# Splitting a weight-conversion step into two moves and laying attention's steps out anew, in a kernel of attention and two feed-forward layers

## The chip, the cores and the metric

The kernel runs on one core of a Trainium2 chip. The metric is the device time of one execution in microseconds; the kernel before was run three times.

## What is computed

The inputs are float64. For each of 8 batches and 8 heads an attention is computed between 512 tokens `x` and 32 states, in both directions; the two results, laid side by side, are 4352 rows of 512. They pass through two feed-forward layers of width 2048, the first with a leaky slope `alpha`, the second with `h - tanh(h)`:

```
xread = softmax(scale * x @ state.T) @ state
sread = softmax(scale * state @ x.T) @ x
x  = concat([xread, sread])              # 8 batches of 512 + 32 rows
h  = x @ w_in;  g = max(h, 0) + alpha * min(h, 0);  x = g @ w_out
h  = x @ w2_in; out = (h - tanh(h)) @ w2_out
```

## The kernel before

**Products in parts.** Each operand of a large product is held as a high and a low part, and a product is three matmuls of 128x512 (`TERMS`, L32).

**The first layer** goes by blocks of 512 rows, one per batch, and by 16 slices `f` of 128 hidden columns; one (block, slice) is a *visit*, and (1,4) below is slice 4 of block 1. `emit_h` (L581) makes the hidden slice: 12 matmuls in block 0, and 6 in blocks 1 to 7, where it reads a product of w_in with the batch's states (`PW`) instead of w_in. `act_a` (L595) makes the activation and its high part `g` (ScalarE L598, VectorE L599, ScalarE L600), `act_b` (L603) the low part (VectorE L604), and `emit_o` (L609) sends the visit *before* through w_out in 12 matmuls (L619). The order of visits is block 0, slices 0 to 7; block 1, slices 0 to 15; block 0, slices 8 to 15; then the other blocks (L1160).

**A visit is a list of places.** Around those calls stand lists of small tasks, kept in `plan` by `at(i, f, place, ...)` (L1018), in this order: `emit_h`, *early*, `act_a`, *gap*, *mid*, `emit_o` of the visit before, *late*, *end* (L1162 to L1183). `act_b` stands between gap and mid in blocks 1 to 7, and behind mid in block 0. Every engine works through its own share of this one order; within a place, tasks run as they were added.

**The conversion** turns the float64 weights of the first layer into two float32 words, 32 jobs of 512 KB (`jobs`, L125). A step (`conv_step`, L176) number t does a phase of five jobs: `conv_a` of job t-1 (ScalarE, L112), `conv_b` of t-2 (VectorE L115, L117, L118, the last one adding the sign, and ScalarE L122), `conv_load` of t (a DMA on SP's queue, L103 or L109), `conv_c` of t-3 (ScalarE copy L159 or L161, GpSimd add L162) and `conv_d` of t-4 (GpSimd subtract L168 or L171, which completes the part). There are 36 steps: six before the first visit, 17 in block 0's first eight visits (two or three in each), 13 in block 1. Raw words lie in a ring of four buffers (tag `raw`); a buffer is free once L118 and L122 have read it. The ring also takes two of the four reads of `PW` for block 1 (L366).

**Attention** of a batch goes by two groups of heads, `a` and `c`, in steps s0 to s6 whose places `timetable` (L1021) lists: transposes on TensorE (s0, s1, s3b, s6), scores (s2), the softmax on VectorE and ScalarE (s2t, s2b, s3, s3x, s4, s4m, s4t), the split into the operand of `emit_h` (s4b) and the states' read (s5). `state_mask` and `state_turn` (L336, L343) prepare the states, `project_one` (L389) makes half a product of w_in with the states: three matmuls into a PSUM tile (L396), high part by ScalarE (L399), low part by VectorE (L400), and two DMAs of 256 KB to memory; `load_parts` (L404) reads them back. All these small products use a PSUM pool of two tiles (`ps_a`, L61), handed out in turn.

Of the kernel before, what the change touches and what calls it, by code (L numbers as in the profile page):

```python
# [35 lines left out]
def attention_and_two_mlps(ctx, tc, x, state, w1_in, w1_out, alpha, w2_in, w2_out, out):  # L36
    nc = tc.nc
    B, H, S, D = x.shape
# [5 lines left out]
    NF = DFF // P  # L44
# [66 lines left out]
    def high_abs(m, r):  # L111
        nc.scalar.activation(m.bitcast(F32), r[:, :, 1].bitcast(F32), AF.Abs)  # L112

    def high_word(m, r):
        nc.vector.tensor_scalar(m.bitcast(F32), m.bitcast(F32), HIGH_MAX, HIGH_MIN,  # L115
                                op0=ALU.min, op1=ALU.max)
        nc.vector.tensor_scalar(m, m, 3, LOW30, op0=ALU.logical_shift_left, op1=ALU.bitwise_and)  # L117
        nc.vector.scalar_tensor_tensor(m, r[:, :, 1], SIGN_TOP, m,  # L118
                                       op0=ALU.bitwise_and, op1=ALU.bitwise_or)

# [6 lines left out]
    raws, words, low, loaded = {}, {}, {}, set()  # L127
# [10 lines left out]
        high_abs(words[k], raws[k])  # L138

    def conv_b(k):  # L140
        r = raws.pop(k)
        high_word(words[k], r)
        low[k] = work.tile([P, DM], I32, tag="cq", name="cq", bufs=3)
        low_word(low[k], r)

# [25 lines left out]
            nc.gpsimd.tensor_tensor(w_out(f, 1), v, w_out(f, 0).bitcast(F32), op=ALU.subtract)  # L171

    ticks = [0]
    phases = [conv_load, conv_a, conv_b, conv_c, conv_d]

    def conv_step():  # L176

        t = ticks[0]
        if t >= 2 * NF + 4:
            return  # L180
        for lead in (1, 2, 0, 3, 4):
            if 0 <= t - lead < 2 * NF:
                phases[lead](t - lead)
        ticks[0] += 1

# [5 lines left out]
    def combine(mat, j, take, ahead):  # L193

        def raw(m, jj):
            got = []
            for h in range(2):
                r, done = take("raw")
                raw_words(r, 1, jj + h * NJ, m)
                got.append((r, done))  # L200
            return got

        got = ahead.pop((mat, j), None)
        if got is None:
            got = raw(mat, j)
        m, m_done, q, q_done = [], [], [], []

        def a(h):
            t, done = take("m")
            m.append(t)  # L210
            m_done.append(done)
            high_abs(t, got[h][0])

        def b(h):
            high_word(m[h], got[h][0])
            t, done = take("q")
            q.append(t)
            q_done.append(done)
            low_word(t, got[h][0])
            got[h][1]()  # L220

        def c(h):
            nc.gpsimd.tensor_tensor(q[h], m[h], q[h], op=ALU.add)  # L223
            m_done[h]()

        a(0)
        yield
        a(1)
        b(0)
        yield  # L230
        b(1)
        c(0)
        yield
        c(1)
        n = (mat, j + 1) if j + 1 < NJ else (mat + 1, 0)
        if n[0] < 2:
            ahead[n] = raw(*n)
        yield "words"
        u, v = (t.bitcast(F32) for t in q)
        s, s_done = take("s")  # L240
        one, two = slice(0, HW), slice(HW, DM)
        sub = partial(nc.gpsimd.tensor_tensor, op=ALU.subtract)

        def parts(src, places):
            n = src.shape[-1]
            o, done = take("o")
            o = o[:, :, :n]
            nc.scalar.copy(o[:, 0], src)  # L248
            yield
            sub(o[:, 1], src, o[:, 0].bitcast(F32))  # L250
            for k, i in enumerate(places):
                nc.sync.dma_start(out=wc_dram[mat][j // 2][i, j % 2], in_=o[:, :, k * HW:(k + 1) * HW].bitcast(F32))
            done()

        if mat == 0:
            nc.gpsimd.tensor_tensor(s[:, one], v[:, one], v[:, two], op=ALU.add)
            sub(v[:, one], u[:, one], v[:, one])
            yield from parts(u, (0, 5))
            sub(s[:, two], v[:, two], v[:, one])
            yield from parts(v, (4, 6))  # L260
            sub(u[:, two], u[:, two], s[:, two])
            yield from parts(s, (1, 2))
            yield from parts(u[:, two], (3,))
        else:
            sub(s[:, one], u[:, one], u[:, two])
            sub(u[:, one], v[:, one], u[:, one])
            yield from parts(v, (3, 5))
            sub(s[:, two], v[:, one], s[:, one])
            yield from parts(u, (4, 0))
            sub(v[:, two], v[:, two], s[:, two])  # L270
            yield from parts(s, (1, 2))
            yield from parts(v[:, two], (6,))
        s_done()
        for done in q_done:
            done()
# [742 lines left out]
    def at(i, f, when, *todo):  # L1018
        plan.setdefault((i, f, when), []).extend(todo)

    def timetable(i, a, c):  # L1021

        if i == 0:
            when = dict(s0=(1, "gap"), s1=(2, "early"), s2=2, s2t=2, s2b=2, s3=2, s3x=(2, "late"),
                        s3b=(3, "early"), s4=3, s4m=3, s4t=3, s4b=(3, "late"), s5=(3, "late"), s6=(4, "late"))
            then = dict(s0=(4, "gap"), s1=(5, "early"), s2=5, s2t=5, s2b=5, s3=5, s3x=(5, "late"),
                        s3b=(6, "early"), s4=6, s4m=6, s4t=6, s4b=(6, "late"), s5=(6, "late"), s6=(7, "late"))
        else:
            def table(first):
                return dict(s0=first, s1=first + 1, s2=first + 2, s2t=(first + 3, "gap"), s2b=first + 3,  # L1030
                            s3=(first + 4, "gap"), s3x=first + 4, s3b=(first + 4, "late"), s4=(first + 5, "gap"),
                            s4m=first + 5, s4t=(first + 6, "gap"), s4b=(first + 6, "late"), s5=first + 6,
                            s6=(first + 7, "late"))
            start = 7 if i + 2 < B else 5
            when, then = (table(0), table(start)) if i > 1 else (table(9), table(8 + NF))
        for g, table in ((a, when), (c, then)):
            for name, w in table.items():
                f, place = w if isinstance(w, tuple) else (w, "mid")

                at(*((i, f) if f < NF else (0, f - NF + (NF // 2 if g is a else 0))), place, getattr(g, name))  # L1040

    with tc.manual_schedule():
        load_next_x()
# [7 lines left out]
        for z in [a.spread, a.s0, a.s1, tick, a.s2, c.spread, a.s2t, c.s0, a.s3, c.s1, a.s3x, c.s2, c.s2t, c.s3,  # L1051
                  a.s4, c.s3x, tick, a.s4m, a.s4t, c.s4, tick, tick, c.s4m, c.s4t, a.r0, a.r1, tick,
                  c.r0, c.r1, slopes, tick, load_next_x, load_next_x]:
            z()
        at(0, 0, "gap", a.s2b)
        at(0, 0, "late", c.s2b)
        at(0, 1, "early", a.s3b, c.s3b)
        at(0, 1, "late", a.s5)
        at(0, 2, "gap", c.s5)
        at(0, 2, "late", a.s6, c.s6)  # L1060
        places = dict(gap=(0, 2, 4, 6), mid=(1, 3, 5, 7), late=(0, 2, 4, 6), end=(0, 1, 3, 5, 7))
        for f, place in ((0, "gap"), (0, "end"), (1, "gap"), (2, "gap"), (2, "end"), (3, "gap"), (4, "gap"), (4, "end"),
                         (5, "gap"), (6, "gap"), (7, "late"), (8, "gap"), (9, "gap")):
            at(1, f, place, tick)
        for place, fs in places.items():
            for f in fs:
                at(0, f, place, tick)
        a = attention(1, 0)
        turns = [(0, 1, 0, (0, "mid"), (1, "early")), (0, 2, 0, (1, "mid"), (2, "early")),
                 (0, 1, 1, (2, "end"), (3, "early")), (0, 2, 1, (3, "mid"), (4, "early"))]  # L1070
        for i in (2, 4, 6):
            turns += [(i, i + 1, 0, (0, "early"), (0, "late")), (i, i + 1, 1, (2, "late"), (3, "late"))]
            if i + 2 < B:
# [13 lines left out]
            at(i, f, "early", partial(state_mask, b, g, True))  # L1087
            at(i, f, "end", partial(state_turn, b, g, scores=False))
        todo = [(1, q, g) for q in range(NF // FQ) for g in range(NG)]
        places = [(0, 4), (0, 5), (0, 7), (1, 0), (1, 2), (1, 3), (1, 5), (1, 6)]  # L1090
        todo += [(b, q, g) for b in (3, 5, 7) for g in range(NG) for q in range(NF // FQ)]
        places += [(0, f) for f in range(8, NF)] + [(2, f) for f in range(NF)]
        for (b, q, g), (i, f) in zip(todo, places):
# [1 line left out]
            at(i, f, "late", partial(project_one, b, q, g, 1))  # L1095
        for k in range(2 * NF // FQ):
            at(*((0, 9 + 2 * k) if k < 4 else (2, 2 * k - 7)), "end", partial(save_w_in, k // 2, k % 2))
        for q, (i, f, place) in enumerate(((0, 6, "early"), (1, 2, "early"), (1, 6, "late"), (1, 9, "late"))):
            at(i, f, place, partial(load_parts, 1, q))
        at(0, 10, "late", load_half_sum)  # L1100
        for i, (blk, n) in enumerate(seq):
# [54 lines left out]
        for f in range(6, NF):  # L1156
            at(B, f, "late", partial(fill.go, 1))

        pend = None
        visits = [(0, f) for f in range(NF // 2)] + [(1, f) for f in range(NF)] + [(0, f) for f in range(NF // 2, NF)]  # L1160
        visits += [(i, f) for i in range(2, len(seq)) for f in range(NF)]
        for i, f in visits:  # L1162
# [4 lines left out]
            g = act_a(n, f, ph)  # L1167
            for z in plan.get((i, f, "gap"), ()):
                z()
            if 0 < i < B:  # L1170
                act_b(n, f, ph, g)
            for z in plan.get((i, f, "mid"), ()):
                z()
            if not 0 < i < B:
                act_b(n, f, ph, g)
            if pend:
                emit_o(*pend)
# [123 lines left out]
```

## Time and profile before

| | us |
|---|---|
| median of three runs | 1522.1 (1518.54 to 1523.98) |
| profiled execution, its own time | 1523.92 |
| span of its instructions | 1522.1 |
| first matmul of visit (0,0) | 29.59 |
| first matmul of visit (1,0) | 118.45 |
| first matmul of visit (1,9) | 192.39 |

The span is what the trace covers; all times of the trace count from its start. An idle time before an instruction is followed by what ended it: `[3.09 <-DMA raw]` is 3.09 us of idle, ended by the landing of a transfer.

### The profile page before, as it was taken

To read this page: it belongs to the slowest core of one execution; us is meant where nothing else is said; L and a number is where in the kernel's file an instruction comes from. 1 tells how busy PE (TensorE), PEld (TensorE's weight loads), DVE (VectorE), ACT (ScalarE), POOL (GpSimd) and SP (SyncE) were. 2 spreads that over 40 slices of the span, in tenths; PEclk is the share of its full clock that TensorE was granted. 3 is DMA by queue.
4 is the path that set the end of the run, shared out by engine and by line. 5 is a ranking of instruction groups with operands and counts; after the bars stand their busy time and mean duration, and the time that the engine had idled before them with its cause. 6 is when DMAs were issued, how large, how long until landed. Compare 5 with 4: busy or idle time off the path is not lost.

```text
span 1522.1 us, 22868 instructions
## 1 busy us (share of the span) xinstructions
PE 1427.7 (94%) x8188; PEld 1194.2 (78%) x8188; DVE 980.7 (64%) x1430; ACT 729.2 (48%) x1322; POOL 530.7 (35%) x414
## 2 busy tenths in 40 slices
PE   5777799989999999999999899999999999999998
PEld 2555577766677677777988687888888989999998
DVE  6876544656577666676445565656347688878874
ACT  4655534444455555555434454545345444444443
POOL 2544400000145445435300211112016387666662
PEclk9998799999999999999999999999999999999999
DMA  6357707795769596758972767272796943443421
GB/s 163 121 167 230 219 2 266 250 318 162 203 189 250 170 263 199 224 172 267 285 223 87 280 208 249 111 271 105 253 344 210 346 132 133 139 139 132 139 84 35
DMA packets 230977, 294.40 MB, mean 193 GB/s; under 512 B 57808, under 2 KB 133584, under 8 KB 229840
## 3 DMA queue, kind: packets, MB, share of 16 engines
q1 hardware_dynamic: 228608, 292.39, 59.9%
q8 instruction: 64, 1.05, 0.3%
q10 hardware_dynamic: 2256, 0.56, 0.2%
q14 instruction: 49, 0.40, 0.1%
HBM read 170.73 MB, written 122.16 MB: 192 GB/s over the span
## 4 chain that ended last, share of the span: by engine, by line
PE 60%; DVE 6%; DMA 5%; ACT 4%; issue 3%; POOL 2%; SPq 1%; ACTq 0%; DVEq 0%; POOLq 0%
PE ps_m L987 20%; PE ps_m L806 17%; PE acc L619 12%; PE ps_h L591 6%; PE ps_m L871 2%; DVE ps_h L599 1%; DVE g L604 1%; PE ps_p L396 1%; ACT g L600 1%; ACT t L598 1%; DMA c_raw<-in_moe_w_in 1%; DMA rx<-y 1%; DMA gt<-g 1%; DMA g<-t 1%; DVE c L823 1%
## 5 line engine op out<-in xcount | busy, mean ns | idle before, releaser
L619 PE MATMUL acc<-g,wo 128*128 128x512 f32 (+1 forms) x1728 | 424.3, 393 | 23.3 <-ACT g L600 12.0
L619 PEld LDWEIGHTS acc<-g,wo 128*128 128x128 f32 x1728 | 316.8, 194 | 110.6 <-DVE g L604 18.7
L987 PE MATMUL ps_m<-wp,s 128*128 128x256 f32 x2856 | 343.0, 282 | 2.9 <-ACT e L970 2.8
L987 PEld LDWEIGHTS ps_m<-wp,s 128*128 128x128 f32 x2856 | 341.4, 190 | 4.6 <-ACT e L970 3.2
L806 PE MATMUL ps_m<-x,ch 128*128 128x512 f32 x1344 | 312.6, 394 | 8.3 <-DVE c L823 4.5
L806 PEld LDWEIGHTS ps_m<-x,ch 128*128 128x128 f32 x1344 | 251.8, 188 | 68.6 <-DVE c L823 6.5
L932 DVE TENSOR_TENSOR s<-gt,s 128x512 fp32r<-128x512 f32 (+1 forms) x216 | 219.4, 1067 | 44.3 <-ACT s L948 43.4
L599 DVE SCALAR_TENSOR_TENSOR ps_h<-ps_h,sign,t 128x512 f32<-128x512 f32 (+1 forms) x144 | 104.8, 727 | 158.3 <-ACT t L598 157.8
L600 ACT ACTIVATE g<-ps_h,sign 128x512 fp32r<-128x512 f32 (+1 forms) x144 | 95.7, 665 | 152.0 <-DVE ps_h L599 152.0
L591 PE MATMUL ps_h<-x,pw 128*128 128x512 f32 x624 | 163.5, 397 | 4.2 <-DMA pw<-pw 4.2
L948 ACT CAST s<-gt 128x512 fp32r<-128x512 f32 (+1 forms) x216 | 120.4, 597 | 88.9 <-PE ps_m L987 37.3
L598 ACT ACTIVATE t<-ps_h,slope 128x512 f32<-128x512 f32 (+1 forms) x144 | 95.7, 664 | 98.9 <-PE ps_h L591 98.6
L604 DVE SCALAR_TENSOR_TENSOR g<-ps_h,sign,g 128x512 fp32r<-128x512 f32 (+1 forms) x144 | 102.7, 713 | 59.5 <-ACT g L600 56.6
L591 PEld LDWEIGHTS ps_h<-x,pw 128*128 128x128 f32 x624 | 114.6, 189 | 29.9 <-issue 5.0
L223 POOL TENSOR_TENSOR c_q<-c_m,c_q 128x512 int32<-128x512 int32 x32 | 42.1, 1315 | 268.6 <-ACT c_q L122 218.9
L817 POOL TENSOR_TENSOR t<-c,t 128x512 f32<-128x512 f32 x32 | 41.6, 1300 | 251.8 <-ACT t L816 224.1
L816 ACT ACTIVATE t<-c 128x512 f32<-128x512 f32 x96 | 60.5, 632 | 123.1 <-DVE c L823 108.7
L823 DVE TENSOR_TENSOR c<-ps_m,c 128x512 f32<-128x512 f32 x96 | 64.7, 685 | 58.7 <-PE ps_m L806 43.2
L250 POOL TENSOR_TENSOR c_o<-c_q,c_o 128x512 fp32r<-128x512 f32 (+1 forms) x48 | 54.4, 1134 | 108.7 <-ACT c_o L248 108.7
L914 POOL TENSOR_TENSOR s<-gt,gt 128x512 f32<-128x512 f32 (+1 forms) x36 | 54.8, 1525 | 84.4 <-DMA gt<-g 83.9
L817 DVE TENSOR_TENSOR t<-c,t 128x512 f32<-128x512 f32 x64 | 53.9, 842 | 46.6 <-ACT t L816 46.6
L162 POOL TENSOR_TENSOR cq<-cm,cq 128x512 int32<-128x512 int32 x32 | 41.6, 1301 | 102.6 <-DVE cm L118 56.2
(138 smaller groups left out, 1643.0 us busy)
## 6 DMA issues: line engine op xcount, KB each, us to landing
g<-t SPq DMA_DIRECT2D x128, 256.0 KB, 2.3
gt<-g SPq DMA_DIRECT2D x64, 512.0 KB, 5.1
wc<-c_o SPq DMA_DIRECT2D x112, 256.0 KB, 3.3
ch<-wc SPq DMA_DIRECT2D x56, 512.0 KB, 7.6
pw<-pw SPq DMA_DIRECT2D x104, 256.0 KB, 5.2
wp<-wc SPq DMA_DIRECT2D x28, 512.0 KB, 7.5
raw<-in_moe_w_in SPq DMA_DIRECT2D x16, 512.0 KB, 4.7
raw<-in_moe_w_out SPq DMA_DIRECT2D x16, 512.0 KB, 5.1
```

The source lines that it names most:

```text
L591: nc.tensor.matmul(ps[:, :n], lhsT=w[i], rhs=xt[:, j, :n], start=(k == 0 and m == 0), stop=(k == len(pairs) - 1 and m == 2))
L598: nc.scalar.mul(t, ph, slope[:, f:f + 1])
L599: nc.vector.scalar_tensor_tensor(ph, ph, sign[:, f:f + 1], t, op0=ALU.mult, op1=ALU.max)
L600: nc.scalar.mul(g[:, 0, :n], ph, sign[:, f:f + 1])
L604: nc.vector.scalar_tensor_tensor(g[:, 1, :n], ph, sign[:, f:f + 1], g[:, 0, :n].bitcast(F32), op0=ALU.mult, op1=ALU.subtract)
L619: nc.tensor.matmul(acc[t][:, :n], lhsT=w[i][:, t * P:(t + 1) * P], rhs=g[:, j, :n], start=(first and k == 0), stop=(last and k == 2))
L806: nc.tensor.matmul(b, lhsT=w[p][:, cc], rhs=XT[key, i][cc][:, q], start=(i not in GOES_ON and cc == k == 0), stop=(cc == 1 and k == 2), sk ...
L817: eng.tensor_tensor(t, h, t, op=ALU.subtract)
L823: nc.vector.tensor_tensor(h, ps[j, i], h, op=ALU.add)
L932: nc.vector.tensor_tensor(made[k - 1][:, 1], src, made[k - 1][:, 0].bitcast(F32), op=ALU.subtract)
L948: nc.scalar.copy(made[k][:, 0], source(blk, i, jj))
L987: nc.tensor.matmul(dst[:, t * HW:(t + 1) * HW], lhsT=s[:, p, r, t * P:(t + 1) * P], rhs=w[:, q], start=first, stop=(jj == NJ // 2 - 1 and ...
```

## The change

The step becomes two moves. The first does L112, L115 and L117 and the load, and the load is now that of job t+1. The second does L118 and L122 (`conv_s`), `conv_c` and `conv_d`. In block 0 each of the first eight visits gets two steps, at early and gap and at late and end; block 1 gets 14 steps over its first eleven visits, two each in slices 2, 3 and 4. `act_b` stands ahead of mid in block 0 too (its slices 8 to 15 included). Batch 1's attention, the states' turns, six of the eight projections for block 1 and its four reads of `PW` are placed elsewhere.

```diff
-    def high_word(m, r):
+    def high_word(m):
...
+    def sign_word(m, r):
         nc.vector.scalar_tensor_tensor(m, r[:, :, 1], SIGN_TOP, m,
...
     def conv_b(k):
+        high_word(words[k])
+
+    def conv_s(k):
         r = raws.pop(k)
-        high_word(words[k], r)
+        sign_word(words[k], r)
         low[k] = work.tile([P, DM], I32, tag="cq", name="cq", bufs=3)
         low_word(low[k], r)
...
-    phases = [conv_load, conv_a, conv_b, conv_c, conv_d]
+
+    def moves(*phases):
+        t = ticks[0]
+        if t < 2 * NF + 4:
+            for phase, lead in phases:
+                if 0 <= t - lead < 2 * NF:
+                    phase(t - lead)
+
+    def conv_step_a():
+
+        moves((conv_a, 1), (conv_b, 2), (conv_load, -1))
+
+    def conv_step_b():
+        moves((conv_s, 2), (conv_c, 3), (conv_d, 4))
+        ticks[0] += 1
 
     def conv_step():
-
-        t = ticks[0]
-        if t >= 2 * NF + 4:
-            return
-        for lead in (1, 2, 0, 3, 4):
-            if 0 <= t - lead < 2 * NF:
-                phases[lead](t - lead)
-        ticks[0] += 1
+        conv_step_a()
+        conv_step_b()
...
         if i == 0:
-            when = dict(s0=(1, "gap"), s1=(2, "early"), s2=2, s2t=2, s2b=2, s3=2, s3x=(2, "late"),
-                        s3b=(3, "early"), s4=3, s4m=3, s4t=3, s4b=(3, "late"), s5=(3, "late"), s6=(4, "late"))
-            then = dict(s0=(4, "gap"), s1=(5, "early"), s2=5, s2t=5, s2b=5, s3=5, s3x=(5, "late"),
-                        s3b=(6, "early"), s4=6, s4m=6, s4t=6, s4b=(6, "late"), s5=(6, "late"), s6=(7, "late"))
+            when = dict(s0=(2, "late"), s1=(3, "early"), s2=(3, "late"), s2t=(3, "end"), s2b=(3, "end"), s3=(3, "end"),
+                        s3x=(4, "gap"), s3b=(4, "late"), s4=(4, "end"), s4m=(4, "end"), s4t=(4, "end"), s4b=(5, "gap"),
+                        s5=(5, "early"), s6=6)
+            then = dict(s0=(5, "late"), s1=(6, "early"), s2=6, s2t=(6, "late"), s2b=(6, "late"), s3=(6, "late"),
+                        s3x=(6, "end"), s3b=7, s4=(7, "early"), s4m=(7, "early"), s4t=(7, "gap"), s4b=7, s5=(7, "late"),
+                        s6=(NF, "late"))
...
+        def halves(i, f, *places):
+            for k, place in enumerate(places):
+                at(i, f, place, (conv_step_a, conv_step_b)[k % 2])
+
+        for f in range(NF // 2):
+            halves(0, f, "early", "gap")
+        for f in range(11):
+            if f in (2, 3, 4):
+                halves(1, f, "early", "gap", "mid", "end")
+            else:
+                halves(1, f, "gap", "end")
         at(0, 0, "gap", a.s2b)
         at(0, 0, "late", c.s2b)
-        at(0, 1, "early", a.s3b, c.s3b)
-        at(0, 1, "late", a.s5)
-        at(0, 2, "gap", c.s5)
-        at(0, 2, "late", a.s6, c.s6)
-        places = dict(gap=(0, 2, 4, 6), mid=(1, 3, 5, 7), late=(0, 2, 4, 6), end=(0, 1, 3, 5, 7))
-        for f, place in ((0, "gap"), (0, "end"), (1, "gap"), (2, "gap"), (2, "end"), (3, "gap"), (4, "gap"), (4, "end"),
-                         (5, "gap"), (6, "gap"), (7, "late"), (8, "gap"), (9, "gap")):
-            at(1, f, place, tick)
-        for place, fs in places.items():
-            for f in fs:
-                at(0, f, place, tick)
+        at(0, 1, "mid", a.s3b, c.s3b)
+        at(0, 2, "mid", a.s5)
+        at(0, 2, "late", c.s5)
+        at(0, 3, "mid", a.s6, c.s6)
         a = attention(1, 0)
-        turns = [(0, 1, 0, (0, "mid"), (1, "early")), (0, 2, 0, (1, "mid"), (2, "early")),
-                 (0, 1, 1, (2, "end"), (3, "early")), (0, 2, 1, (3, "mid"), (4, "early"))]
+        turns = [(0, 1, 0, (0, "mid"), (1, "late")), (0, 2, 0, (1, "late"), (2, "early")),
+                 (0, 1, 1, (3, "mid"), (4, "early")), (0, 2, 1, (3, "late"), (4, "late"))]
...
-        places = [(0, 4), (0, 5), (0, 7), (1, 0), (1, 2), (1, 3), (1, 5), (1, 6)]
+        places = [(0, 4), (0, 5), (1, 0), (1, 1), (1, 3), (1, 4), (1, 6), (1, 7)]
...
-        for q, (i, f, place) in enumerate(((0, 6, "early"), (1, 2, "early"), (1, 6, "late"), (1, 9, "late"))):
+        for q, (i, f, place) in enumerate(((0, 7, "early"), (1, 2, "late"), (1, 6, "early"), (1, 9, "early"))):
             at(i, f, place, partial(load_parts, 1, q))
...
+        for f in range(NF // 2):
+            halves(0, f, "late", "end")
...
-            if 0 < i < B:
+            if i < B:
                 act_b(n, f, ph, g)
             for z in plan.get((i, f, "mid"), ()):
                 z()
-            if not 0 < i < B:
+            if i == B:
                 act_b(n, f, ph, g)
```

## Rows read from the trace of the kernel before

**Rows 1.** The page: busy tenths of TensorE, and its granted clock, in 40 slices.

```profile
PE   5777799989999999999999899999999999999998
...
PEclk9998799999999999999999999999999999999999
```

**Rows 2.** Busy time by stretch: first the column heads, then three stretches.

```profile
core 0: us, PE busy (x) PEld busy (x) DVE busy (x) ACT busy (x) POOL busy (x), PEclk, DMA share, GB/s
...
29.59:118.45 88.86, 65.80 (x376) 47.75 (x375) 73.10 (x132) 53.91 (x103) 46.30 (x36) 0.88 0.49 144
118.45:192.39 73.94, 57.20 (x194) 43.22 (x195) 45.54 (x70) 37.60 (x66) 32.42 (x26) 0.83 0.76 231
...
295.00:315.00 20.00, 17.21 (x75) 12.36 (x74) 9.19 (x16) 7.53 (x15) 0.00 (x0) 1.00 0.97 344
```

**Rows 3.** TensorE's longest wait in block 0's stretch, 29 to 118.4: us, times, longest.

```profile
PE ps_p L396 <- DVE wide L554: 4.4, 1, 4.4
```

**Rows 4.** TensorE's waits in block 1's stretch, 118.4 to 192.4.

```profile
PE ps_p L396 <- DVE pe L400: 7.0, 2, 4.7
PE acc L619 <- DVE g L604: 4.4, 3, 1.9
PE ps_h L591 <- DMA pw<-pw: 4.2, 2, 2.8
PE ps_w L569 <- DVE wi L400: 2.6, 1, 2.6
```

**Rows 5.** ScalarE's waits for raw words, in block 1's stretch.

```profile
ACT cm L112 <- DMA raw<-in_moe_w_out: 11.4, 5, 3.2
...
ACT cm L112 <- DMA raw<-in_moe_w_in: 2.9, 2, 1.5
```

**Rows 6.** Timeline: one load's issue, and ScalarE's wait for its landing.

```profile
136.84 0.53 SPq L109 DMA_DIRECT2D raw<-in_moe_w_out  x1
...
142.06 0.66 ACT L112 ACTIVATE cm<-raw 128x512 f32<-128x512 f32 x1 [3.09 <-DMA raw<-in_moe_w_out]
```

**Rows 7.** Groups by line and shape, 0 to 200 us: total, mean ns.

```profile
L115 DVE TENSOR_SCALAR cm<-cm 128x512 f32<-128x512 f32 x32 | 23.3, 728 | 0.0
L118 DVE SCALAR_TENSOR_TENSOR cm<-raw,cm 128x512 int32<-128x512 int32 x32 | 23.1, 722 | 1.1
...
L117 DVE TENSOR_SCALAR cm<-cm 128x512 int32<-128x512 int32 x32 | 19.4, 607 | 1.1
...
L400 DVE TENSOR_TENSOR wi<-ps_p,wi 128x512 fp32r<-128x512 f32 x8 | 5.5, 688 | 4.5 <-ACT wi L399 4.4
```

**Rows 8.** Timeline: L115 beside a GpSimd instruction, then L115 and L117 alone.

```profile
106.58 1.29 POOL L168 TENSOR_TENSOR wi<-cq,wi 128x512 fp32r<-128x512 f32 x1
106.80 1.35 DVE L115 TENSOR_SCALAR cm<-cm 128x512 f32<-128x512 f32 x1
...
114.62 0.42 DVE L115 TENSOR_SCALAR cm<-cm 128x512 f32<-128x512 f32 x1
...
115.08 0.43 DVE L117 TENSOR_SCALAR cm<-cm 128x512 int32<-128x512 int32 x1
```

**Rows 9.** Timeline: groups of 12 matmuls, at the high clock and behind an idle time.

```profile
97.75 3.00 PE L619 MATMUL acc<-g,wo 128*128 128x512 f32 x12
...
187.51 5.01 PE L619 MATMUL acc<-g,wo 128*128 128x512 f32 x12
```

**Rows 10.** DMA issues: KB each, median us from issue to landing.

```profile
raw<-in_moe_w_out SPq DMA_DIRECT2D x16, 512.0 KB, 5.1
...
wo<-pw SPq DMA_DIRECT2D x8, 256.0 KB, 8.2
```

**Rows 11.** Waits after the stretches, 192 to 420 us: TensorE's longest.

```profile
PE acc L619 <- ACT g L600: 3.1, 1, 3.1
```

**Rows 12.** Timeline: visit (0,7), its hidden slice on TensorE and its activation on VectorE.

```profile
101.27 3.07 PE L591 MATMUL ps_h<-x,wi 128*128 128x512 f32 x12
...
113.97 0.75 DVE L599 SCALAR_TENSOR_TENSOR ps_h<-ps_h,sign,t 128x512 f32<-128x512 f32 x1
```

More of the change, by code (lines that the diff above doesn't have):

```diff
@@ L214, in b @@
         def b(h):
-            high_word(m[h], got[h][0])
+            high_word(m[h])
+            sign_word(m[h], got[h][0])
             t, done = take("q")
@@ L1038, in timetable @@
                 f, place = w if isinstance(w, tuple) else (w, "mid")
-                at(*((i, f) if f < NF else (0, f - NF + (NF // 2 if g is a else 0))), place, getattr(g, name))
+                if f >= NF:
+                    j, f = (1, f - NF) if i == 0 else (0, f - NF + (NF // 2 if g is a else 0))
+                    at(j, f, place, getattr(g, name))
+                else:
+                    at(i, f, place, getattr(g, name))
     with tc.manual_schedule():
@@ L1054, in attention_and_two_mlps @@
             z()
+        def halves(i, f, *places):
[6 more added lines that the diff above has]
+                halves(1, f, "early", "gap", "mid", "end")
+            else:
+                halves(1, f, "gap", "end")
         at(0, 0, "gap", a.s2b)
         at(0, 0, "late", c.s2b)
-        at(0, 1, "early", a.s3b, c.s3b)
-        at(0, 1, "late", a.s5)
-        at(0, 2, "gap", c.s5)
-        at(0, 2, "late", a.s6, c.s6)
-        places = dict(gap=(0, 2, 4, 6), mid=(1, 3, 5, 7), late=(0, 2, 4, 6), end=(0, 1, 3, 5, 7))
-        for f, place in ((0, "gap"), (0, "end"), (1, "gap"), (2, "gap"), (2, "end"), (3, "gap"), (4, "gap"), (4, "end"),
-                         (5, "gap"), (6, "gap"), (7, "late"), (8, "gap"), (9, "gap")):
-            at(1, f, place, tick)
-        for place, fs in places.items():
-            for f in fs:
-                at(0, f, place, tick)
+        at(0, 1, "mid", a.s3b, c.s3b)
+        at(0, 2, "mid", a.s5)
+        at(0, 2, "late", c.s5)
+        at(0, 3, "mid", a.s6, c.s6)
         a = attention(1, 0)
-        turns = [(0, 1, 0, (0, "mid"), (1, "early")), (0, 2, 0, (1, "mid"), (2, "early")),
-                 (0, 1, 1, (2, "end"), (3, "early")), (0, 2, 1, (3, "mid"), (4, "early"))]
+        turns = [(0, 1, 0, (0, "mid"), (1, "late")), (0, 2, 0, (1, "late"), (2, "early")),
+                 (0, 1, 1, (3, "mid"), (4, "early")), (0, 2, 1, (3, "late"), (4, "late"))]
         for i in (2, 4, 6):
```

## The prediction
> **What bounds the kernel now.** I read the page's slices first. TensorE is busy nine tenths almost everywhere behind slice 5, and in the first five slices 5 to 7 tenths, at a granted clock below full [rows 1]. So whatever this change can win lies in the first 190 us, where the conversion runs. The view by stretch splits them [rows 2]. Block 0's stretch (A, 29.59 to 118.45, 88.86 us): VectorE is busy 73.10, TensorE 65.80, the transfers 0.49. Block 1's (B, 118.45 to 192.39, 73.94 us): TensorE 57.20, VectorE 45.54, transfers 0.76. A is a stretch of VectorE, with TensorE waiting for its products, the longest of these waits 4.4 us [rows 3]. B belongs to no engine: TensorE idles 73.94 - 57.20 = 16.7 us, mostly for VectorE's low parts of projections (7.0) and of g (4.4) [rows 4], while VectorE itself is idle 28 us. The view of ScalarE's waits names the root: it stands 11.4 + 2.9 = 14.3 us at L112 for raw words that have not landed [rows 5]. One load is issued at 136.84 and L112 starts at 142.06, behind 3.09 us of idle [rows 6]; a load takes 5.1 us to land [rows 10] and has one step of lead. ScalarE works in order, so the activation and the projection's high part (L399) queue behind that L112, VectorE's L400 behind L399, and TensorE behind the two `ps_a` tiles.
>
> **Part by part, stretch A.** Sixteen steps instead of 17: one step's L115, L117, L118 go, 0.73 + 0.61 + 0.72 = 2.06 us of VectorE [rows 7]. The projection pair of (0,7) goes to B: 2 x 0.69 = 1.38 [rows 7], six matmuls and four stores with it. L115 takes 0.42 alone and 1.35 when a GpSimd instruction has just begun, L117 0.43 alone [rows 8]; against the means of 0.728 and 0.607 [rows 7] that is 0.31 + 0.18 = 0.49 us lost per step. GpSimd's two instructions start right behind a step's L118. In the new order the first step of a visit still follows the last sign at once; the second (late) has L604, the mid tasks and often a wait in between. I take half the loss away: 8 x 0.49 = 3.9. Bounds: nothing, and all of it, 16 x 0.49 = 7.8. The Trainium skill, "SBUF — State Buffer", "Who interferes with whom", has a rule for it: a `tensor_scalar` in a two-port mode and a GpSimd instruction exclude each other for a whole instruction, and the order of issue decides who stands. By that rule alone the late step collides as well whenever L122 is late and GpSimd starts late with it; then nothing is saved, and the sum below would come to 1511. The pair of rows agrees with the lock.
>
> VectorE's work in A is then 73.1 - 2.1 - 1.4 - 3.9 = 65.7. Its idle time is 15.8 now. Walking the new order with these durations I find TensorE still waiting: in (0,1) the turn waits for the copy of s3b's transposes (some 2 us), in (0,4) the second projection for L400 of the first (some 3), in (0,5) s0 for the low part of a projection that now stands behind s4b's split (some 4), in (0,7) s5 for the copy of c's s3b (some 3); L604 ahead of mid lets `emit_o` start without a wait everywhere. So VectorE's idle grows rather than shrinks: I take 18. A = 65.7 + 18 = 83.7, **5 us less**. Bounds: VectorE without idle is 65.7 (23 less, unreached by any stretch here); with the waits of the last rival, 7 more than before.
>
> **Stretch B.** The load moves from step t to step t-1's first move. It must wait for the buffer of four jobs earlier, which L118 and L122 of the step before release, so the lead grows from one step to nearly two: at B's pace of one step in 4 to 6 us that is over the 5.1 us of a landing; in slices 2 to 4, with two steps a visit, some 6 us, just enough. The waits at L112 then go, and with them the 7.0 and nearly all of the 4.4; 2.6 (s6 behind a projection) shrinks as well. I leave 2 us of these. Wait for `PW`, 4.2 at slice 8: its read moves from (1,6) late to (1,6) early, but its second half needs a raw buffer that step 31's second move at (1,6) end releases, and SP stands on it with the stores of (1,6)'s projections behind, whose staging tiles slice 7's L399 needs; I keep 2. The read for slice 4 moves from (1,2) early to (1,2) late, and such reads take 8.2 us [rows 10]; two visits of some 6 us less the wait for its buffers leave it 3.5 late. New waits and old: 2 + 2 + 3.5 = 7.5 us instead of 16.7.
>
> B's work: 9 visits of 6 + 12 matmuls and ten projections of three are 192 of 0.25 us [rows 9], 48 us; what is left of the 57.20, 9 us, is the lower clock, which shows behind idle times: twelve matmuls in 5.01 instead of 3.00 [rows 9], the engine having waited twice for `PW` just before [rows 4]; the granted clock of B is 0.83 of the 2.4 GHz level [rows 2]. With two projections more the work is 49.9, and the clock's loss goes with the idle, 9 x 7.5 / 16.7 = 4. ScalarE, busy 37.60 over 13 steps and ten projections [rows 2], gets two steps a visit in slices 2 to 4 and sets the pace there: an estimate of 1 us. B = 49.9 + 7.5 + 4 + 1 = 62.4, and 1.5 for landings that lengthen when the transfers are busier: 64, **10 us less**. Floor: transfers of 0.76 x 73.94 = 56 us at a full share, which another stretch nearly reaches (0.97) [rows 2], 18 less; ceiling: as before.
>
> **Behind B.** In block 0's slices 8 to 15 `act_b` changes places with a projection's L400. The longest waits there are 3.1 us for g's high part [rows 11], which L604 does not touch; I take 0, between 3 less and 3 more. Six steps before the first visit keep their order; only SP issues job 6's load ahead of batch 1's x, which nothing needs before (0,2): 0.
>
> **Sum.** 5 + 10 = 15 us off the profiled execution's 1523.9 is 1509; that execution stands 1.8 above the median of 1522.1, so I forecast **1507**.
>
> **Rivals.** (1) *Transfers take the lead back* (0.22). B moves 231 GB/s in 74 us; in 64 it is 267, at a share of 0.76 x 74 / 64 = 0.88. Landings stretch, L112 waits again, half of B's gain goes and A gives little: 8 off, 1514. For it: the 8.2 us of the reads; against it: 344 GB/s in one stretch [rows 2].
> (2) *The lead is nominal* (0.13). The ring has four buffers. If VectorE runs late, L118 of the previous step sets the issue, not the place, and the load comes no earlier than now; A keeps its length since VectorE's work hardly falls. 1520. For it: VectorE is full in A; against it: idle 28 of 74 in B.
> (3) *Slower: batch 1's second group ends in A's last visit* (0.10). Its split stood in (0,6) late, and now stands in (0,7) mid; `emit_h` of (1,0) needs it. In (0,7) VectorE already runs 12.7 us behind TensorE (113.97 against 101.27) [rows 12]. If that lag is kept, behind L599 follow a sign, s4t, L604, the split and s5, about 4 us of VectorE plus 3 of ScalarE turns: (1,0) starts 7 us later than now. It decides the sum once the lag at (0,6) exceeds some 6 us and rival 2 holds in B as well: 1522 + 7 = 1529.
>
> **Chances.** Forecast 0.55, rivals 0.22, 0.13, 0.10. 0.3% is 4.6 us, about what a measurement of this kernel can tell from no change. Faster takes the forecast and nearly all of rival 1: 0.75; the same, rival 2 and little else: 0.14; slower 0.11. The range reaches from 1497 (half the collisions more, B near 59: 25 off) to 1521, taking in rivals 1 and 2 and leaving out the slower one.
>
> **What would show it.** Right: L112's waits for raw words in B fall from 14.3 to under 4; (1,0) starts near 113 and (1,9) near 178; L396's wait for L400 in B under 2; L115's mean falls to about 0.6; a new wait for `PW` at slice 4. Wrong: L112 still waits over 8 us (rivals 1, 2), (1,0) starts behind 118 (rival 3), or the stretch behind (1,9) changes by more than 3 us.

## The result, and the profile after

The changed kernel takes 1510.5 us (median of 8 runs, 1504.5 to 1514.0) against 1523.8 for the kernel before on the same chips (8 runs): a ratio of **0.9911, 95% interval 0.9891 to 0.9930**, 13.3 us off. Forecast was 1507, 15 us below the 1522.1 known then. The profiled execution took 1510.4, its span is 1508.6.

Line numbers shift: L605 is `emit_h`, L633 `emit_o`, L612 to L614 and L618 the activation, L120 the sign, L124 the low word, L410 a projection's matmuls, L413 and L414 its high and low part, L416 its stores, L423 the read of the product, L340 and L341 the split of s4b, L460 attention's transposes, L558 s5, L361 a turn, L167, L173 and L176 GpSimd's add and its two subtracts.

The page's slices, to lay beside [rows 1]:

```profile
PE   5868899999899999999999899999999999999998
...
PEclk9998999999999999999999999999999999999999
```

Busy time by stretch, cut at the same visits as [rows 2]: (0,0) to (1,0), which is A, and (1,0) to (1,9), which is B. The third and fourth rows cut B at (1,2) and (1,5).

```profile
core 0: us, PE busy (x) PEld busy (x) DVE busy (x) ACT busy (x) POOL busy (x), PEclk, DMA share, GB/s
29.37:114.01 84.64, 62.91 (x370) 46.13 (x368) 69.64 (x124) 51.82 (x99) 44.44 (x34) 0.90 0.51 152
114.01:174.80 60.79, 52.65 (x200) 39.93 (x201) 55.56 (x73) 37.96 (x66) 30.41 (x24) 0.89 0.84 254
...
128.79:151.13 22.34, 17.79 (x67) 13.54 (x66) 22.10 (x28) 15.06 (x26) 13.86 (x11) 0.85 1.00 285
151.13:174.80 23.67, 20.29 (x86) 15.43 (x85) 20.47 (x25) 14.47 (x26) 10.88 (x9) 1.00 0.80 254
```

A lost 4.2 us (88.86 to 84.64) and B 13.2 (73.94 to 60.79); with 0.2 from the start, TensorE reaches (1,9) 17.6 us earlier. Some of it is given back: 1.5 in visit (1,9) itself, where the conversion still runs (TensorE reaches (1,10) 16.1 earlier). Visit (2,0) starts 15.8 earlier, block 2's slice 4 14.6, and the end comes 13.5 earlier. TensorE's granted clock in B went from 0.83 to 0.89.

TensorE's waits in A, and its two longest in B, against [rows 3, 4]:

```profile
PE ps_xt L460 <- DVE wi L414: 4.1, 1, 4.1
PE ps_r L558 <- ACT e2t L530: 3.9, 1, 3.9
...
PE ps_p L410 <- DVE wi L414: 3.2, 1, 3.2
...
PE ps_st L361 <- ACT e2t L530: 2.2, 1, 2.2
```

```profile
PE ps_h L605 <- DMA wo<-pw: 5.2, 4, 3.9
PE acc L633 <- DVE g L618: 1.9, 1, 1.9
```

In B the 7.0 us behind L400 and the 2.6 behind s6's projection are gone, and a wait for the read of the product is new (3.9 at slice 4, followed there by another of 0.65). Later in B, SP stands on the read for slice 8, and ScalarE then waits for a staging tile of the projections, because the stores that free such tiles stand behind that read:

```profile
160.19 6.84 SPq L423 DMA_DIRECT2D pw<-pw  x4
...
171.08 0.59 ACT L413 CAST pe<-ps_p 128x512 fp32r<-128x512 f32 x1 [3.39 <-DMA pw<-pe]
```

ScalarE's wait for raw words in B, 14.3 us in [rows 5], is one row:

```profile
ACT cm L112 <- DMA raw<-in_moe_w_out: 2.1, 1, 2.1
```

VectorE's share of the conversion in B, with L120 where L118 stood:

```profile
L117 DVE TENSOR_SCALAR cm<-cm 128x512 int32<-128x512 int32 x12 | 13.8, 1152 | 0.4
L115 DVE TENSOR_SCALAR cm<-cm 128x512 f32<-128x512 f32 x12 | 11.6, 963 | 0.0
L120 DVE SCALAR_TENSOR_TENSOR cm<-raw,cm 128x512 int32<-128x512 int32 x12 | 10.3, 859 | 0.1
```

L115 and L117 together take 2.11 us a step here, where the kernel before needed 0.850 + 0.508 = 1.36 in its B and [rows 8] show 0.85 alone. The same two groups in A, before and after, and one L117 of B beside a GpSimd add:

```profile
L117 DVE TENSOR_SCALAR cm<-cm 128x512 int32<-128x512 int32 x18 | 11.5, 641 | 0.6
L115 DVE TENSOR_SCALAR cm<-cm 128x512 f32<-128x512 f32 x17 | 11.5, 678 | 0.0
```

```profile
L117 DVE TENSOR_SCALAR cm<-cm 128x512 int32<-128x512 int32 x17 | 13.2, 776 | 0.6
...
L115 DVE TENSOR_SCALAR cm<-cm 128x512 f32<-128x512 f32 x16 | 7.2, 447 | 0.3 <-ACT cm L112 0.3
```

```profile
131.04 1.35 POOL L167 TENSOR_TENSOR cq<-cm,cq 128x512 int32<-128x512 int32 x1 [2.89 <-DVE cm L120]
...
131.27 1.40 DVE L117 TENSOR_SCALAR cm<-cm 128x512 int32<-128x512 int32 x1
```

### The profile page after: what moved, and what is told of

Read it like the earlier page. It is cut to its first block, busy times and chain, and to the rows that moved or that the text cites. A ratio compares the mean times of both kernels' runs of the same rounds, so it can differ in the third digit from the quotient of the medians.

```text
span 1508.6 us, 22873 instructions
## 1 busy us (share of the span) xinstructions
PE 1422.1 (94%) x8188; PEld 1192.1 (79%) x8188; DVE 991.6 (66%) x1430; ACT 729.7 (48%) x1322; POOL 532.1 (35%) x414
## 5 line engine op out<-in xcount | busy, mean ns | idle before, releaser
L633 PE MATMUL acc<-g,wo 128*128 128x512 f32 (+1 forms) x1728 | 416.2, 388 | 20.8 <-ACT g L614 11.8
L633 PEld LDWEIGHTS acc<-g,wo 128*128 128x128 f32 x1728 | 312.2, 191 | 104.0 <-ACT g L614 16.6
L614 ACT ACTIVATE g<-ps_h,sign 128x512 fp32r<-128x512 f32 (+1 forms) x144 | 95.8, 666 | 160.5 <-DVE ps_h L613 160.5
L605 PE MATMUL ps_h<-x,pw 128*128 128x512 f32 x624 | 162.7, 396 | 0.9 <-DMA pw<-pw 0.9
L618 DVE SCALAR_TENSOR_TENSOR g<-ps_h,sign,g 128x512 fp32r<-128x512 f32 (+1 forms) x144 | 102.6, 713 | 62.1 <-ACT g L614 58.9
L612 ACT ACTIVATE t<-ps_h,slope 128x512 f32<-128x512 f32 (+1 forms) x144 | 95.7, 664 | 88.3 <-PE ps_h L605 88.0
L605 PEld LDWEIGHTS ps_h<-x,pw 128*128 128x128 f32 x624 | 114.4, 188 | 26.1 <-issue 1.3
L837 DVE TENSOR_TENSOR c<-ps_m,c 128x512 f32<-128x512 f32 x96 | 64.7, 685 | 58.9 <-PE ps_m L820 43.2
L167 POOL TENSOR_TENSOR cq<-cm,cq 128x512 int32<-128x512 int32 x32 | 42.0, 1313 | 95.7 <-DVE cm L120 60.5
```

The source lines that it names most:

```text
L605: nc.tensor.matmul(ps[:, :n], lhsT=w[i], rhs=xt[:, j, :n], start=(k == 0 and m == 0), stop=(k == len(pairs) - 1 and m == 2))
L612: nc.scalar.mul(t, ph, slope[:, f:f + 1])
L614: nc.scalar.mul(g[:, 0, :n], ph, sign[:, f:f + 1])
L618: nc.vector.scalar_tensor_tensor(g[:, 1, :n], ph, sign[:, f:f + 1], g[:, 0, :n].bitcast(F32), op0=ALU.mult, op1=ALU.subtract)
L633: nc.tensor.matmul(acc[t][:, :n], lhsT=w[i][:, t * P:(t + 1) * P], rhs=g[:, j, :n], start=(first and k == 0), stop=(last and k == 2))
L837: nc.vector.tensor_tensor(h, ps[j, i], h, op=ALU.add)
```

## The experiments

Theory L, the prediction's: ScalarE's waits for raw words drag on the activation and the projections, and the longer lead of the loads is most of the gain. Rival V: the loads were covered, and the split, the low part ahead of mid and the new places did it. Each run's ratio is to the kernel before on the same chip. Stretches are single profiled executions. How far such profiles differ by themselves can be seen behind (2,0), which hardly any edit touches: that span took 1236.1 us before, 1238.4 after, and 1237.2 to 1242.9 in the other profiles. A differs by some 2 us as well: two runs below that change nothing ahead of (1,1) took 82.7 and 83.8 us for it, the changed kernel 84.6.

**The lead alone, put back and put in.**

```diff
-        moves((conv_a, 1), (conv_b, 2), (conv_load, -1))
+        moves((conv_a, 1), (conv_b, 2), (conv_load, 0))
```

> The changed kernel with each step's load put back to job t (one step of lead); all else as changed. Theory L (the longer lead is what shortened block 1's stretch, 73.9 to 60.8 us): ScalarE's waits for raw words in that stretch come back from 2.1 to over 8 us, the stretch takes 67 to 72 us, block 0's stays near 84.6, and the time is 7 to 11 us above the changed kernel. Rival V (the split of the step, the low part and the new layout did it; the loads were covered): the stretch stays within 2 us of 60.8 and the time within 3 us of the changed kernel.

```diff
-        for lead in (1, 2, 0, 3, 4):
+        for lead in (1, 2, -1, 3, 4):
             if 0 <= t - lead < 2 * NF:
-                phases[lead](t - lead)
+                phases[max(lead, 0)](t - lead)
```

> The kernel before with one edit: a step loads job t+1 instead of job t, in the same place. Theory L: ScalarE's 14.3 us of waits for raw words in block 1's stretch fall under 5, the stretch goes from 73.9 to 62 to 67 us, block 0's (88.9) loses up to 4, as 5.0 us of such waits stand there too; the time falls 8 to 13 us. Rival V: block 1's stretch stays over 71 us and the time within 3 us of before.

With the lead put back: 1516.6, ratio 0.9945 (0.9926 to 0.9963), some 5 us above the changed kernel by the ratios. ScalarE's waits for raw words in B, and the stretch:

```profile
ACT cm L112 <- DMA raw<-in_moe_w_out: 9.2, 5, 3.3
ACT cm L112 <- DMA raw<-in_moe_w_in: 3.4, 2, 1.7
```

```profile
115.36:180.06 64.70, 53.01 (x205) 39.83 (x201) 55.89 (x73) 38.06 (x67) 30.78 (x24) 0.89 0.79 238
```

With the lead alone in the kernel before: 1514.1, ratio 0.9928 (0.9908 to 0.9949), 11 us off. Its waits in B, and its two stretches:

```profile
ACT cm L112 <- DMA raw<-in_moe_w_out: 2.3, 4, 0.9
```

```profile
29.53:117.16 87.63, 67.78 (x377) 49.45 (x375) 71.31 (x131) 53.93 (x103) 46.19 (x36) 0.86 0.53 153
117.16:178.21 61.05, 50.30 (x194) 39.09 (x195) 47.82 (x70) 37.66 (x66) 32.79 (x26) 0.92 0.91 271
```

One number in the old kernel takes ScalarE's waits in B from 14.3 us to 2.3 and the stretch from 73.94 to 61.05, all that the whole change reaches there. So L's mechanism holds, and V's "covered" is refuted. But the first run is a miss for L, and lies between the two: the raw-word waits come back nearly in full (12.6 us), yet B takes 64.7, not 67 to 72, and the time rises by 5 us, not 7 to 11. Without the lead the other parts still take 8 us off. The two ways shorten the same idle time and do not add: 11 + 8 is more than the 13 of both. TensorE's idle time in B was 16.7 us before, and is 11.7 with the lead put back, 10.8 with the lead alone and 8.1 with both; its waits for a projection's low part there (7.0 + 2.6) are 4.9, 5.1 and none that the list shows. By the intervals the lead alone cannot be told from the whole change.

**The low part behind mid again** in block 0.

```diff
-            if i < B:
+            if 0 < i < B:
                 act_b(n, f, ph, g)
...
-            if i == B:
+            if not 0 < i < B:
                 act_b(n, f, ph, g)
```

> The changed kernel with the low part of the activation behind mid again in block 0. Theory L gives this edit little: block 0's stretch 1 to 3 us longer (its output products wait for that part again, as 1.7 us did before), slices 8 to 15 of block 0 within 2 us, the time 0 to 4 above the changed kernel. Rival V: block 0's stretch 4 us longer or more, that is as long as before the change, and the time 4 to 8 us above.

1509.8, ratio 0.9903 (0.9878 to 0.9927): no difference that these runs can tell from the changed kernel. A takes 82.45 us, B 61.98. This part of the change carries nothing measurable; V's 4 us are refuted, and L's "1 to 3 longer" is not seen either (A's 2.2 us less is about what profiles differ by there).

**The words whole**: L115 and L117 back beside the sign.

```diff
-        moves((conv_a, 1), (conv_b, 2), (conv_load, -1))
+        moves((conv_a, 1), (conv_load, -1))
...
-        moves((conv_s, 2), (conv_c, 3), (conv_d, 4))
+        moves((conv_b, 2), (conv_s, 2), (conv_c, 3), (conv_d, 4))
```

> The changed kernel with L115 and L117 moved into the second move, right ahead of the sign; load, absolute value and all else stay. If the split spreads VectorE's conversion so that it meets GpSimd less, L115 and L117 (together 1.22 us in block 0's stretch, 2.11 in block 1's) get longer and both stretches with them, 3 to 6 us in all. If the split is what makes them meet GpSimd in block 1's stretch (1.36 together before the change), they fall back to about 1.4 there, VectorE's busy time there falls from 55.6 to 47 to 50, and the stretch is the same or up to 3 us shorter.

1510.3, ratio 0.9907 (0.9881 to 0.9932), the time of the changed kernel. The stretch and the two groups in B:

```profile
112.21:172.58 60.37, 51.49 (x204) 38.83 (x201) 45.86 (x74) 37.89 (x67) 29.98 (x24) 0.92 0.86 260
```

```profile
L115 DVE TENSOR_SCALAR cm<-cm 128x512 f32<-128x512 f32 x12 | 8.0, 670 | 0.0
L117 DVE TENSOR_SCALAR cm<-cm 128x512 int32<-128x512 int32 x12 | 8.0, 669 | 0.4
```

The second branch is right: 1.34 us a step instead of 2.11, VectorE's busy time in B down 9.7 us, the stretch 0.4. The split is what makes VectorE meet GpSimd there, and ten microseconds of VectorE's busy time in B were worth nothing that these runs can tell: it is not what paces B. The busy time counts L117 as busy while it stands beside GpSimd.

**The old layout** of attention, turns, projections and reads, with the new conversion and low part. The edit takes back the change's lines of `timetable`, of batch 0's steps, `turns`, `places` and `load_parts`; the last of them:

```diff
...
-        places = [(0, 4), (0, 5), (1, 0), (1, 1), (1, 3), (1, 4), (1, 6), (1, 7)]
+        places = [(0, 4), (0, 5), (0, 7), (1, 0), (1, 2), (1, 3), (1, 5), (1, 6)]
...
-        for q, (i, f, place) in enumerate(((0, 7, "early"), (1, 2, "late"), (1, 6, "early"), (1, 9, "early"))):
+        for q, (i, f, place) in enumerate(((0, 6, "early"), (1, 2, "early"), (1, 6, "late"), (1, 9, "late"))):
```

> The changed kernel with attention's steps, the states' turns, the projections and their reads back where they were before the change; the conversion's two moves and the activation's low part as changed. If the longer lead of the loads is the whole gain (the kernel before with that edit alone ran at 1514), this runs at 1511 to 1516 and block 1's stretch takes 59 to 64 us, block 0's 85 to 89. If the new layout carries a share of its own, block 0's stretch goes back to 88 us or more and the time to 1515 or more.

1514.8, ratio 0.9937 (0.9914 to 0.9959): the first branch by the time and by A, and just outside it by B (65.1 against 59 to 64). A takes 86.23 us (84.64 with the new layout), B 65.08 (60.79); in B TensorE waits 6.0 us for L414 at s6 and 5.9 at the projections, the waits of [rows 4]. The layout's share is about 4 us by the ratios, most of it in B, where it keeps s6 and the projections off each other; the waits show it, the time does not, since the intervals of the two kernels overlap. Against the kernel before with the lead alone (1514.1, B 61.1), this run has the new steps of the conversion and the new place of the low part as well, and is no faster: on the old layout these two brought nothing that the runs show.

**The three waits left, and who takes them over.** First the read for slice 4, then the products behind which TensorE waits in A, then both with the words whole.

```diff
-        ((0, 7, "early"), (1, 2, "late"), (1, 6, "early"), (1, 9, "early"))
+        ((0, 7, "early"), (1, 1, "end"), (1, 6, "early"), (1, 9, "early"))
```

> The changed kernel with the read of the product for slices 4 to 7 of block 1 issued at (1,1) end instead of (1,2) late. If the 3.9 us wait for it at slice 4 is what it costs, block 1's stretch (60.8 us) takes 55 to 58 us and the time falls 3 to 5. If ScalarE and VectorE, which run behind there, set the pace anyway, the wait goes over to a later slice and the stretch stays within 2 us of 60.8.

```diff
-                        s3x=(4, "gap"), s3b=(4, "late"), s4=(4, "end"), s4m=(4, "end"), s4t=(4, "end"), s4b=(5, "gap"),
+                        s3x=(4, "late"), s3b=(4, "late"), s4=(4, "end"), s4m=(4, "end"), s4t=(4, "end"), s4b=(5, "late"),
...
-                        s3x=(6, "end"), s3b=7, s4=(7, "early"), s4m=(7, "early"), s4t=(7, "gap"), s4b=7, s5=(7, "late"),
+                        s3x=(6, "end"), s3b=7, s4=(7, "early"), s4m=(7, "early"), s4t=(7, "gap"), s4b=7, s5=(NF, "early"),
```

> The changed kernel with three of attention's steps put later: the first group's s3x from (0,4) gap to late, its s4b from (0,5) gap to late, the second group's s5 from (0,7) late to (1,0) early. The waits of 3.2 us in (0,4), 4.1 in (0,5) and 3.9 in (0,7) are each for a result queued behind one of these. If they cost what they show, block 0's stretch (84.6 us) takes 74 to 79; if VectorE's backlog (69.6 us busy in it) sets the pace, 81 to 85 and the waits stand elsewhere.

The third has both of these edits and that of the whole words.

> The edits of the two runs before together, and L115 and L117 moved right ahead of the sign (which took 10 us off VectorE's busy time in block 1's stretch and nothing measurable off the time). If VectorE's backlog is what holds either edit back, the three together give more than their sum: block 0's stretch 72 to 77, block 1's 52 to 57, the time 1497 to 1502. If the transfers hold block 1 (0.84 of their time at 60.8 us), its stretch stays over 57 and the time at 1501 to 1506.

1512.4 (0.9916, 0.9895 to 0.9936), 1509.1 (0.9895, 0.9875 to 0.9916) and 1509.2 (0.9902, 0.9872 to 0.9931): none is faster than the changed kernel by more than the intervals. B takes 64.1, 63.0 and 64.2 us, longer than the 60.8 of the changed kernel; the first run misses both of its branches by that, and the third by its time. Each edit removed or shortened its wait and found another. In the first, SP stands on the read until its stores are there, the next raw loads stand behind it, ScalarE waits for raw words, and TensorE for the projection that ScalarE should have read:

```profile
129.30 6.13 SPq L423 DMA_DIRECT2D wo<-pw  x4
...
135.52 1.02 SPq L109 DMA_DIRECT2D raw<-in_moe_w_out  x2
...
139.97 0.66 ACT L112 ACTIVATE cm<-raw 128x512 f32<-128x512 f32 x1 [3.27 <-DMA raw<-in_moe_w_out]
...
146.97 1.65 PE L410 MATMUL ps_p<-wi,snp 128*128 128x512 f32 x3 [7.49 <-DVE pe L414]
```

In the second, (1,0) starts at 110.8 instead of 114.0, and TensorE waits there for the read for slice 0, which left SP at 104.4:

```profile
104.43 2.56 SPq L423 DMA_DIRECT2D wo<-pw  x4
...
110.75 0.98 PE L605 MATMUL ps_h<-x,wo 128*128 128x512 f32 x3 [4.54 <-DMA wo<-pw]
```

**The reads moved to where SP waits anyway.**

```diff
-        ((0, 7, "early"), (1, 2, "late"), (1, 6, "early"), (1, 9, "early"))
+        ((0, 7, "early"), (1, 2, "early"), (1, 6, "early"), (1, 9, "early"))
```

> The changed kernel with the read for slices 4 to 7 issued at (1,2) early, between the two raw loads of that visit: behind (1,1) end SP stood 6.1 us on that read, for its stores, with two raw loads behind it. If SP's order is what moved the wait there, a place where the next load must wait for its buffer anyway costs it nothing: the 3.9 us wait at slice 4 falls under 2, TensorE does not wait over 3 us for L414 in block 1's stretch, and that stretch takes 57 to 59 us against 60.8. If the transfers themselves hold the stretch, it stays within 1.5 us of 60.8 with the wait at another place.

In the next two the words are whole and the read for slice 0 stands at (0,6) early as well; the first of them also has the products behind, by the edit shown above.

```diff
-        ((0, 7, "early"), (1, 2, "late"), (1, 6, "early"), (1, 9, "early"))
+        ((0, 6, "early"), (1, 2, "early"), (1, 6, "early"), (1, 9, "early"))
```

> The three later steps of attention and the words whole again, with the read for slice 4 at (1,2) early and the read for slice 0 at (0,6) early instead of (0,7) early. With the steps alone TensorE reached (1,0) 3.3 us earlier and waited 4.5 us there for that read. If the reads were what ate those gains, (1,0) starts at 106 to 110, (1,9) at 166 to 170, and the time is 1501 to 1505. If not, (1,9) stays at 173 or later and the time at 1507 or more.

> As the run before without the three later steps of attention: the two reads moved, the words whole. If the reads are the larger share, (1,0) starts at 110 to 113, block 1's stretch takes 56 to 59 us and the time is 1503 to 1507; if the steps of attention are, the time is within 2 us of the changed kernel.

1511.0 (0.9914, 0.9894 to 0.9935), 1510.3 (0.9911, 0.9896 to 0.9926) and 1510.0 (0.9910, 0.9893 to 0.9926). All three fall in the branches that forecast no gain. In the first, the wait at slice 4 fell only from 3.9 to 2.5, and B took 61.7. With the products behind as well, (1,0) starts at 108.1, 6 us earlier than in the changed kernel, and (1,9) at 174.9, as there (174.8). Most of that gain was never there: only the first three matmuls of (1,0) run early, the others need the second group's split and wait for it until 112.90, and TensorE reaches (1,1) 1.7 us earlier than in the changed kernel (121.3 against 123.0) and (1,2) 1.5 earlier.

```profile
108.08 0.84 PE L605 MATMUL ps_h<-x,wo 128*128 128x512 f32 x3
...
112.90 0.51 PE L605 MATMUL ps_h<-x,wo 128*128 128x512 f32 x1 [3.98 <-ACT x L340]
```

What is left is lost between (1,2) and (1,5): 25.0 us instead of 22.3, with the transfers at 0.95 of their time (1.00 in the changed kernel's shorter window).

**Less to carry in that window**, on top of the run with reads, products and whole words: a step of the conversion and the loads of the next block's activation are moved out of slices 2 to 4.

```diff
-            if f in (2, 3, 4):
+            if f in (2, 4, 5):
...
-                    for j, f in (((1, 2), (1, 4)), ((0, 9), (0, 15)))[i] if i < 2 else ((i, 6), (i, 13)):
+                    for j, f in (((1, 5), (1, 7)), ((0, 9), (0, 15)))[i] if i < 2 else ((i, 6), (i, 13)):
```

> The run with the reads and products moved, and less to carry in slices 2 to 4 of block 1: the visits with two conversion steps are 2, 4 and 5 instead of 2, 3 and 4, and the two loads of the next batch's x go from (1,2) and (1,4) to (1,5) and (1,7). The transfer engines were busy 0.95 to 1.00 of the time from (1,2) to (1,5), which took 22.3 us in the changed kernel and 25.0 in that run, whose start at (1,0) was 6 us earlier and whose (1,9) was not. If the transfers' full time there ate the gain, (1,2) to (1,5) takes 19 to 22 us, (1,9) starts at 168 to 171, and the time is 1503 to 1507. If something else paces block 1, (1,9) stays at 173 or later and the time over 1508.

1509.3, ratio 0.9902 (0.9876 to 0.9927). The window from (1,2) to (1,5) took 22.5 us instead of 25.0, short of the forecast, and (1,9) still came at 175.4; TensorE was 1.7 us ahead of the changed kernel at (1,5) and behind it at (1,9). Between them lie slices 6 to 8, with a stand of SP that the changed kernel has too. SP stands 6.5 us here on the read for slice 8, whose second buffer the conversion's step at (1,6) end must free; the stores of (1,6)'s projections stand behind it, and slice 7's L413 waits for their staging tile:

```profile
160.26 6.49 SPq L423 DMA_DIRECT2D pw<-pw  x4
...
166.80 1.07 SPq L416 DMA_DIRECT2D pw<-pe  x2
...
170.60 0.59 ACT L413 CAST pe<-ps_p 128x512 fp32r<-128x512 f32 x1 [3.18 <-DMA pw<-pe]
```

So what fills slices 2 to 4 is one link of what paces block 1: the transfers, or the step of ScalarE, VectorE and GpSimd that this edit moved out with them, which the run does not separate. SP's order around the raw ring may be another: in the changed kernel and in all nine runs that keep its order and the longer lead L413 waits some 4 us for staging tiles, and none of them moved the read for slice 8. In these nine (1,9) starts between 172.6 and 177.3, though (1,0) starts anywhere from 107.8 to 115.5 and (1,1) from 119.0 to 123.1. What a layout free of both links would reach was not tried.

## Why the prediction was right, and where it was not

**The cause** was read rightly: L112's waits for raw words, an in-order ScalarE, L400 and `ps_a` behind it. The waits fell from 14.3 to 2.1 us, L396's wait for L400 in B from 7.0 to none that the list shows, and the edit alone gives 11 of the 13 us. The prediction put B's gain down to the lead; with the new layout in place it is worth only about 5, as the run with the lead put back shows.

**Stretch A**, 83.7 forecast, 84.64 measured: the new waits were foreseen one by one, 2, 3, 4 and 3 us against 2.2, 3.2, 4.1 and 3.9. The terms beneath were not: VectorE is busy 69.6 us, not 65.7, and idle 15.0, not 18; two errors of opposite sign, so that A came out right is partly luck.

**The term that failed is the collisions with GpSimd.** "I take half the loss away" was 3.9 us; L115 and L117 in A went from 1.32 a step (0.678 + 0.641) to 1.22 (0.447 + 0.776), which is 1.6 us, and in B, where the prediction gave them nothing, from 1.36 to 2.11. That is 2.3 of the 3.9 us by which VectorE is busier in A; another 0.7 is the second L400 of (0,7), which the prediction took out of A though in the kernel before it had already run behind (1,0). In B the two instructions meet GpSimd more often, because they often stand where the add or the subtract that the sign before them released has just begun. The pair takes 0.85 us alone, 2.11 in the split order, 1.34 with the words whole. The rule of the Trainium skill, "SBUF — State Buffer", "Who interferes with whom", that the order of issue decides and the loser stands for a whole instruction, agrees with these three numbers. The alternative that the prediction worked out by that rule, nothing saved in A and 1511 in all, was nearer on the collisions; that 1511 is also near the measured 1510.5 is luck, since A came out within 1 us of the forecast all the same.

**Stretch B**, 64 forecast, 60.8 measured. The new wait at slice 4 was 3.5 us forecast, 3.9 measured; the one at slice 8, taken at 2, was 0.9. The 2 us left for other waits were 1.9. The miss is in the terms beside these waits: TensorE was busy 52.65 us, not 49.9 + 4 (198 matmuls at 0.25 are 49.5, so 0.4 of it is a slip of the sum), and idle 8.1, not 7.5 + 1 + 1.5 with ScalarE's pace and longer landings. The transfers ran at 0.84 against the 0.88 of rival 1. Before slice 2 the projections' stores landed in 2.0 us, as in the kernel before (2.1); in slices 2 to 4, at 1.00, they took over 5, and the raw loads of w_out 5.7 against 5.4 (medians).

**Behind B** the prediction took 0 between 3 less and 3 more; the stretch behind (1,9) grew by 4.1 us (1329.7 to 1333.8), which is outside these bounds and over the 3 us that the prediction itself had named as a sign of being wrong. Of it 1.5 lie in visit (1,9), where L618 stands behind L115 and L117 of a conversion step, which the prediction had not looked at; with the words whole that visit takes 4.8 us instead of 6.2, nearly the 4.7 of the kernel before. The span behind (2,0) is 2.3 us longer after, which is within what the profiles differ by there, so little can be said of it. A miss of 3.2 us of opposite sign in B made the total right to 3.5 us; that is luck.

**The signs.** The waits at L112 and at `ps_p`, (1,0) and the wait for `PW` came as named; (1,9) came 3 us earlier. L115's mean fell from 728 to 656 ns over the first 200 us, near the 0.6 named, but L117's rose from 607 to 944, so the sign came true while what it stood for did not.

**The rivals.** Rival 1 (transfers) came true in part and only where two steps share a visit: L112's one wait of 2.1 us is at slice 4. Rival 2 (a nominal lead) is refuted by the lead alone. Rival 3 did not happen: (1,0) came at 114.0, behind a wait of 3.9 us for s5, not 7 us later than before. But the chain it named is there: once s5 and the read for slice 0 were put out of the way, (1,0) waited 4.0 us for the second group's split.

## What to carry to other kernels

A load that lands just after its step on an in-order engine holds up everything that engine does for others, so look first at what an engine off the critical path waits for. What such a wait costs depends on the rest: 12.0 us less of it took 12.9 us off the stretch in the old layout, and 10.5 us less took 3.9 off in the new one. Give such a load another step of lead before moving anything else; here one number gave most of what the whole change gave, and two remedies for the same idle time did not add. When a wait is moved, look at what stands behind the new place on the same queue: a DMA issued early that must wait for its data or its buffer holds every load and store behind it (6.1 us of SP's queue in one run here). And when a stretch starts earlier, look whether its second instruction does too.

## What the runs showed that I had not expected

Nearly ten microseconds of VectorE's time in block 1 (55.6 to 45.9 us busy) changed the stretch by 0.4 us, though VectorE was busy 22.10 of 22.34 us from (1,2) to (1,5): with it freed, the same window took 23.2. Of six microseconds that block 1's first matmul gained (108.1 against 114.0), 1.7 were left one visit later, behind a wait for the other half of the same visit's operand, and none nine visits later. The busy share of an engine, even a full one, did not tell what freeing it was worth; the runs did.
